# Natural Q by a transposing DMA: a two-block attention backward kernel on one core

## The chip, the core and the metric

The kernel runs on one core of one Trainium2 chip. The metric is the device time of one execution in microseconds. The core has a matrix engine (TensorE, PE in the profile, its weight loads PEld), a vector engine (VectorE, DVE), an activation engine (ScalarE, ACT), a general engine (GpSimd, POOL) and a sync engine (SyncE, SP) that here does nothing but issue DMAs. Sixteen DMA engines move the data between HBM (the chip's main memory) and SBUF (the on-chip buffer, 128 partitions). Matmuls write to PSUM, a small accumulator memory of eight banks, and ScalarE or VectorE must copy ("evict") the result from there into SBUF. A matmul contracts over the partitions of its two operands, so an operand whose contracted dimension lies along the free axis must first be transposed. That can be done by TensorE, with a matmul against an identity matrix and an eviction, or by a DMA that transposes.

## The reference

Two independent attention blocks, A and B, of the same shape: 8 batches (B), 96 queries (Sq), model width 640 (D), 32 heads (H), 512 keys (Sk), head width 128 (Dh), all in bfloat16. The kernel computes the forward output and the gradients of all ten inputs.

```
def _A_ref(x, k_cache, v_cache, wq, wo):
    q = (x @ wq).reshape(B, Sq, H, Dh).transpose(0, 2, 1, 3)
    scores = jnp.einsum("bhqd,bhkd->bhqk", q, k_cache) * (Dh ** -0.5)
    p = softmax(scores, axis=-1)
    o = jnp.einsum("bhqk,bhkd->bhqd", p, v_cache)
    return o.transpose(0, 2, 1, 3).reshape(B, Sq, H * Dh) @ wo
...
_out, _vjp = jax.vjp(_f, A_x, A_k_cache, ..., B_wo)   # _f: both blocks, joined on the last axis
return (_out, *_vjp(grad_out))
```

## The kernel before

One program does block A and then block B. Within a block it runs over the 32 heads, and within a head over the 8 batches. A head and batch together are a chunk; there are 2 x 32 x 8 = 512 chunks, and 64 heads counted through both blocks (head 8 here is the ninth head of block A, head 32 the first of block B).

**Order of the work.** The order is written by hand, in ticks. Each head h starts at tick `tick0 + 8 h`, and chunk b of it at one tick later each. Small functions are added to an emitter with a tick and a slot in the tick (lines 505 to 543) and run in that order. The table OFF (line 45) tells at which tick after its start a chunk's steps come, and HK (line 46) at which tick a head's steps come. The tile framework then gives each engine its own fixed queue of instructions, with semaphore waits where data or a buffer is not ready. Each engine takes its queue strictly in order, the sync engine's DMAs too: a DMA that waits holds all that stand behind it.

**A chunk**, by ticks: load K and V, 128 KB each, by the sync queue (`c_ld`, L235; 11 K buffers, 8 V buffers); transpose both on TensorE and evict them together (`c_s1`, L249, L251, L253); scores S = Q K^T (`c_s2a`, L265), row maximum, exponential (L277) and normalisation into P (L287, L296, GpSimd); transpose P, output O^T (`c_s45`, L312, L321); dV from P and natural dO (`c_s4`, L338), evicted by ScalarE into one of six dV_sb tiles (L340) and stored by the sync queue (L341); dP and the row sums, dS (`c_s6`, L360 to L364); dK from dS and natural Q (`c_s7`, L404), evicted (L406) and stored by the sync queue (L407); transpose dS, dQ^T (`c_s78`, L378, L387).

"Natural" means with the queries on the partitions. dK contracts over the queries, so it needs natural Q, while the scores need Q^T.

**A head** adds: the loads of its slice of wq and of wo, the latter transposed by a DMA (`pA`, L179, L181); Q^T and dO^T for all eight batches, two halves of 384 columns each (`pC`, L215, ticks -3 to 0); natural dO at ticks 1 and 2 and natural Q at ticks 3 and 4, by four TensorE transposes into a PSUM bank and one VectorE eviction for each half (`pD`, L231, L232, L170 in `evac`); a transposing DMA for wq^T (`pW`, L195); and, some ten ticks after the head began, two transposing DMAs of O^T and dQ^T (`qA`, L416, targets Onat and dQnat) followed by the weight gradients dwo (`qB`, L430) and dwq (`qD`, L450). All the transposing DMAs, all loads of K and V and all stores of dK and dV stand in the sync queue: 36 issues for a head. The wq loads and the weight gradients' stores go by GpSimd's queue.

**A group** is eight heads. When its last head is through, wo for the group is loaded (`gW`, L462, 1280 KB) and the output projections of the forward output and of dx run over 26 ticks (`gU`, L481), spread between the chunks of the next group's first heads. So of each eight heads some three or four carry projection matmuls, and the others ("plain heads") do not; the first group of all carries none. A group's results are summed in SBUF, and the last group of a block writes them out through four `ob` tiles (L491 to L493).

Of the kernel before, what the change touches and what calls it, by code (L numbers as in the profile page):

```python
# [11 lines left out]
BF16 = mybir.dt.bfloat16  # L12
# [28 lines left out]
SL_HEAD = 90  # L41
# [1 line left out]
SL_SETUP = 96  # L43

OFF = dict(ld=0, s1=2, s2=3, s3=3, s4=4, s5=5, s6=6, s7=7, s8=8)
HK = dict(pA=-6, pB=-4, pW=4, pC0=[-3, -2], pC1=[-1, 0], pD1=[1, 2], pD0=[3, 4], qA0=13, qA1=16, qB=[17, 18], qD=[(19, 0, 2), (20, 2, 4), (21, 4, 5)])
EV = dict(pB0="act", pB1="dve", pC00="act", pC01="act", pC10="act", pC11="dve", pD0="dve", pD1="dve", qA0="dve", qA1="dve", qB0="act", qB1="act", gU="act")
PRIO_OFF = 2000
GSPREAD = 26
# [3 lines left out]
def build_block(tc, em, tick0, blk, x, kc, vc, wq, wo, g_all, out_all, dx, dk, dv, dwq, dwo, ident, ones, pools, HG=8, first=True, groups=None):  # L53
    nc = tc.nc
    B, Sq, D = x.shape
    _, H, Sk, Dh = kc.shape
    assert Dh == 128 and Sk % 128 == 0 and D % 128 == 0
    T = B * Sq
# [3 lines left out]
    KC = Sk // 128  # L62
# [22 lines left out]
    const, ps, kvp, wk, hd, hst, grp = (pools[k] for k in ("const", "ps", "kvp", "wk", "hd", "hst", "grp"))  # L85

    def bank(shape, dt, name):
        return ps.tile(shape, dt, name=name, tag="bank")
# [3 lines left out]
    HS = pools["HS"]  # L92
# [72 lines left out]
    def evac(eng, dst, src, sc=None):  # L165
        if eng == "act":
            nc.scalar.activation(dst, src, ACT.Identity, scale=(1.0 if sc is None else sc))
        else:
            if sc is None:
                nc.vector.tensor_copy(dst, src)  # L170
            else:
                nc.vector.tensor_scalar(dst, src, float(sc), None, op0=ALU.mult)
# [12 lines left out]
    def pB(h):  # L185
        def f():
            st = HS[(blk, h)]
            st["QT_h"] = hd.tile([128, T], BF16, name="QT_h")
            st["dOT_h"] = hd.tile([128, T], BF16, name="dOT_h")
        return f  # L190

    def pW(h):
        def f():
            wqT_h = hst.tile([128, 1, D], BF16, name="wqT_h")
            tc.keep_in_program_order(nc.sync.dma_start_transpose(wqT_h[:], wq[:, h * 128:(h + 1) * 128]))  # L195
            HS[(blk, h)]["wqT_h"] = wqT_h[:, 0]
        return f

    def pC(h, which, si):
        def f():  # L200
            st = HS[(blk, h)]
            (t0, w) = tsplits[si]
            if which == 0:
                dst = st["QT_h"]
                lhs = lambda c: st["wq_h"][:, c, :]
                rhsT = S["xT"]
                sc = scale
            else:
                dst = st["dOT_h"]
                lhs = lambda c: st["woT_h"][:, c, :]  # L210
                rhsT = S["gT"]
                sc = None
            q_ps = bank([128, w], F32, "q_ps")
            for c in range(DC):
                nc.tensor.matmul(q_ps[:], lhs(c), rhsT[:, c, t0:t0 + w], start=(c == 0), stop=(c == DC - 1))  # L215
            evac(EV["pC%d%d" % (which, si)], dst[:, t0:t0 + w], q_ps[:], sc)
        return f

    def pD(h, which, half):
        def f():  # L220
            st = HS[(blk, h)]
            src = st["QT_h"] if which == 0 else st["dOT_h"]
            name = "Qnat_h" if which == 0 else "dOnat_h"
            if half == 0:
                st[name] = hd.tile([Sq, B * 128], BF16, name=name)
            b0 = half * HB
            nb = B - b0 if half else HB
            n_ps = bank([Sq, 8 * 128], BF16, "n_ps")
            for i in range(nb):
                b = b0 + i  # L230
                nc.tensor.transpose(n_ps[:, i * 128:(i + 1) * 128], src[:, b * Sq:(b + 1) * Sq], ident[:])  # L231
            evac(EV["pD%d" % which], st[name][:, b0 * 128:(b0 + nb) * 128], n_ps[:, 0:nb * 128])  # L232
        return f

    def c_ld(h, b):  # L235
# [22 lines left out]
    def c_s2a(h, b):  # L258
        def f():
            with tc.high_priority(PRIO_OFF):  # L260
                st = CS[(blk, h, b)]
                hs = HS[(blk, h)]
                tok = slice(b * Sq, (b + 1) * Sq)
                S_ps = bank([Sq, Sk], F32, "S_ps")
                nc.tensor.matmul(S_ps[:], hs["QT_h"][:, tok], st["KT"], start=True, stop=True)  # L265
                negm = wk.tile([Sq, 1], F32, name="negm", bufs=3)
                nc.vector.tensor_reduce(negm[:], S_ps[:], axis=AX.X, op=ALU.max, negate=True)  # L267
                st["S_ps"], st["negm"] = S_ps, negm
        return f
# [61 lines left out]
    def c_s4(h, b):  # L331
        def f():
            st = CS[(blk, h, b)]
            hs = HS[(blk, h)]
            P_sb = st["P_sb"]
            dV_ps = bank([128, KC * 128], F32, "dV_ps")
            for c in range(KC):
                nc.tensor.matmul(dV_ps[:, c * 128:(c + 1) * 128], P_sb[:, c * 128:(c + 1) * 128], hs["dOnat_h"][:, b * 128:(b + 1) * 128], start=True, stop=True)  # L338
            dV_sb = wk.tile([128, KC * 128], BF16, name="dV_sb", bufs=6)
            nc.scalar.activation(dV_sb[:], dV_ps[:], ACT.Identity, scale=1.0)  # L340
            nc.sync.dma_start(dv[b, h].rearrange("(p c) d -> p (c d)", c=KC), dV_sb[:])  # L341
        return f
# [54 lines left out]
    def c_s7(h, b):  # L397
        def f():
            st = CS[(blk, h, b)]
            hs = HS[(blk, h)]  # L400
            dS_sb = st["dS_sb"]
            dK_ps = bank([128, KC * 128], F32, "dK_ps")
            for c in range(KC):
                nc.tensor.matmul(dK_ps[:, c * 128:(c + 1) * 128], dS_sb[:, c * 128:(c + 1) * 128], hs["Qnat_h"][:, b * 128:(b + 1) * 128], start=True, stop=True)  # L404
            dK_sb = wk.tile([128, KC * 128], BF16, name="dK_sb", bufs=6)
            nc.scalar.activation(dK_sb[:], dK_ps[:], ACT.Identity, scale=1.0)  # L406
            nc.sync.dma_start(dk[b, h].rearrange("(p c) d -> p (c d)", c=KC), dK_sb[:])  # L407
        return f
# [62 lines left out]
    def gU(g, which, t, gi):  # L471
        def f():
            acc = S.get("out_acc" if which == 0 else "dx_acc")
            dst_flat = out_flat if which == 0 else dx_flat
            (c0, w) = gsplits[gi]
            o_ps = bank([128, w], F32, "o_ps")
            for hh in range(groups[g]):
                h = GH0[g] + hh
                src = HS[(blk, h)]["OT_h"] if which == 0 else HS[(blk, h)]["dQT_h"]
                rhs = G[g]["wo_r"][:, hh, c0:c0 + w] if which == 0 else HS[(blk, h)]["wqT_h"][:, c0:c0 + w]  # L480
                nc.tensor.matmul(o_ps[:], src[:, t * 128:(t + 1) * 128], rhs, start=(hh == 0), stop=(hh == groups[g] - 1))  # L481
            if NG == 1:
                ob = wk.tile([128, w], BF16, name="ob", bufs=4)
                evac(EV["gU"], ob[:], o_ps[:])
                nc.gpsimd.dma_start(dst_flat[t * 128:(t + 1) * 128, c0:c0 + w], ob[:])
            elif g == 0:
                evac(EV["gU"], acc[:, t, c0:c0 + w], o_ps[:])
            elif g < NG - 1:
                nc.vector.tensor_tensor(acc[:, t, c0:c0 + w], o_ps[:], acc[:, t, c0:c0 + w], op=ALU.add)
            else:  # L490
                ob = wk.tile([128, w], BF16, name="ob", bufs=4)  # L491
                nc.vector.tensor_tensor(ob[:], o_ps[:], acc[:, t, c0:c0 + w], op=ALU.add)
                (nc.gpsimd if first else nc.sync).dma_start(dst_flat[t * 128:(t + 1) * 128, c0:c0 + w], ob[:])  # L493
        return f
# [4 lines left out]
    for g in range(NG):  # L499
        h0 = GH0[g]  # L500
        for hh in range(groups[g]):
            h = h0 + hh
            c0t = tick0 + h * B
            em.add(c0t + HK["pA"], SL_LOAD, pA(h))
            em.add(c0t + HK["pB"], SL_HEAD, pB(h))
            em.add(c0t + HK["pW"], SL_HEAD, pW(h))
            for si in range(NTS):
                em.add(c0t + HK["pC0"][min(si, len(HK["pC0"]) - 1)], SL_HEAD, pC(h, 0, si))
                em.add(c0t + HK["pC1"][min(si, len(HK["pC1"]) - 1)], SL_HEAD, pC(h, 1, si))
            for half in range(2):  # L510
                em.add(c0t + HK["pD1"][half], SL_HEAD, pD(h, 1, half))
                em.add(c0t + HK["pD0"][half], SL_HEAD, pD(h, 0, half))
            for b in range(B):
                ct = c0t + b
                em.add(ct + OFF["ld"], SLOTS["LOAD"], c_ld(h, b))
# [143 lines left out]
```

## Time and profile before

| | before |
|---|---|
| device time, median of 3 runs | 1777.6 us (1771.38 to 1781.83) |
| profiled execution | 1778.72 us |
| its span, first to last instruction | 1776.9 us |
| mean granted TensorE clock | 0.995 of full |
| DMA | 370.73 MB, mean 209 GB/s, 508657 packets, of which 230000 under 512 B |
| Onat and dQnat transposes, issue to landing, median | 3.8 us (64 of each) |
| TensorE transposes of Q (L231, from QT_h) | 512, mean record 219 to 223 ns |
| evictions of natural Q (L170) | 128, mean 410 ns |

The profile is of one execution. Engines' busy times are unions of their instructions' records. A TensorE record covers the pipeline from the first operand to the last result, so records overlap, and what a matmul takes of the engine is the distance from its start to the next one's. The page counts no busy time for issuing DMAs; that is seen in the sync queue's own timeline, where the duration of an entry is the time the queue needs to hand over one DMA. "DMA share" is the mean share of time in which the 16 DMA engines have packets in flight; it can pass 1 where packets overlap. The chain of waits follows back what released the last instruction, and the clock column tells which share of TensorE's full clock was granted.

### The profile page before, as it was taken

The numbers are of one execution on the slowest core, as the hardware profiler recorded it, in microseconds if no ns is written. First come the engines' busy times: TensorE is split into PE (matmuls) and PEld (weight loads), VectorE is DVE, ScalarE is ACT, GpSimd is POOL, SyncE is SP. The second block draws the span as 40 slices with busy tenths as digits, with TensorE's granted clock in tenths as the row PEclk, the third lists the DMA queues.
The fourth block names the chain that finished last, engine by engine and source line by source line (L and its number), as shares of the span: only waits on it lengthen the run. The fifth ranks groups of instructions, "written<-read, shape, count | busy, mean of one in ns | idle before, by whom it ended". The sixth has DMA issues, their size and how long they took to land.

```text
span 1776.9 us, 65815 instructions
## 1 busy us (share of the span) xinstructions
PE 1752.8 (99%) x24538; PEld 1476.6 (83%) x24538; DVE 1449.4 (82%) x3106; ACT 1470.3 (83%) x4081; POOL 717.1 (40%) x1260
## 2 busy tenths in 40 slices
PE   8999899999999999999899999999999999999998
PEld 6888788888888888888788888888888888888886
DVE  7888766888878887788687888668987788878894
ACT  5999788899778987798777999789987799877992
POOL 2444433444334443345344444334443344433441
PEclk9999999999999999999899999999999999999999
DMA  8889975899858896689997799678896788867874
GB/s 212 220 221 221 240 191 167 206 217 237 210 168 214 217 245 186 178 209 223 236 254 188 211 222 248 186 178 208 221 245 183 182 219 225 238 179 174 222 215 128
DMA packets 508657, 370.73 MB, mean 209 GB/s; under 512 B 230000, under 2 KB 497136, under 8 KB 508336
## 3 DMA queue, kind: packets, MB, share of 16 engines
q1 hardware_dynamic: 493072, 319.82, 70.5%
q0 software_dynamic: 15264, 46.71, 8.8%
q8 instruction: 192, 3.15, 0.8%
q14 instruction: 129, 1.06, 0.2%
HBM read 160.10 MB, written 159.12 MB: 180 GB/s over the span
## 4 chain that ended last, share of the span: by engine, by line
PE 97%; DMA 2%; DVE 1%; issue 0%; ACT 0%; POOL 0%; SPq 0%; ACTq 0%; DVEq 0%; POOLq 0%
PE q_ps L215 12%; PE o_ps L481 12%; PE dK_ps L404 6%; PE dV_ps L338 6%; PE kvT_ps L249 6%; PE kvT_ps L251 6%; PE dP_ps L360 6%; PE S_ps L265 6%; PE dwq_ps L450 6%; PE dwo_ps L430 6%; PE dq_dst_ps L387 5%; PE optp_ps L321 5%; PE optp_ps L312 5%; PE dq_dst_ps L378 5%; PE n_ps L231 4%; DMA xT<-in_B_x_dram 1%
## 5 line engine op out<-in xcount | busy, mean ns | idle before, releaser
L296 POOL TENSOR_SCALAR P_sb<-E_sb,rinv 96x512 bf16<-96x512 bf16 x512 | 352.3, 688 | 680.6 <-DVE rinv L287 674.7
L277 ACT ACTIVATE E_sb<-S_ps,negm 96x512 bf16<-96x512 f32 x512 | 348.7, 681 | 152.1 <-DVE negm L267 151.4
L364 DVE SCALAR_TENSOR_TENSOR dS_sb<-dP_ps,dl_ps,P_sb 96x512 bf16<-96x512 f32 x512 | 384.7, 751 | 106.6 <-PE dl_ps L362 97.6
L267 DVE TENSOR_REDUCE negm<-S_ps 96x1 f32<-96x512 f32 x512 | 348.2, 680 | 56.7 <-PE S_ps L265 55.1
L253 DVE COPY KVT<-kvT_ps 128x1024 bf16<-128x1024 bf16 x512 | 348.5, 681 | 18.5 <-PE kvT_ps L251 6.3
L406 ACT ACTIVATE dK_sb<-dK_ps 128x512 bf16<-128x512 f32 x512 | 302.9, 592 | 51.9 <-PE dK_ps L404 48.5
L340 ACT ACTIVATE dV_sb<-dV_ps 128x512 bf16<-128x512 f32 x512 | 315.6, 616 | 0.0
L327 ACT ACTIVATE PT_sb<-optp_ps 128x384 bf16<-128x384 bf16 x512 | 254.3, 497 | 0.0
L350 POOL TENSOR_TENSOR prod<-OT_h,dOT_h 128x96 bf16<-128x96 bf16 x512 | 186.8, 365 | 106.4 <-ACT OT_h L324 87.4
L249 PE MATMUL kvT_ps<-ident,K_sb 128*128 128x128 bf16 x2048 | 198.4, 219 | 0.0
L251 PE MATMUL kvT_ps<-ident,V_sb 128*128 128x128 bf16 x2048 | 198.4, 219 | 0.0
L404 PE MATMUL dK_ps<-Qnat_h,dS_sb 96*128 96x128 bf16 x2048 | 198.4, 219 | 0.0
L338 PE MATMUL dV_ps<-dOnat_h,P_sb 96*128 96x128 bf16 x2048 | 198.1, 219 | 0.0
L265 PE MATMUL S_ps<-KVT,QT_h 128*96 128x512 bf16 x512 | 194.3, 380 | 1.2 <-DVE KVT L253 1.2
L360 PE MATMUL dP_ps<-KVT,dOT_h 128*96 128x512 bf16 x512 | 195.5, 382 | 0.0
L249 PEld LDWEIGHTS <-K_sb 128*128 128x128 bf16 x2048 | 152.1, 98 | 37.2 <-issue 2.0
L389 DVE COPY dST_sb<-dq_dst_ps 128x384 bf16<-128x384 bf16 x512 | 178.9, 349 | 2.1 <-PE dq_dst_ps L387 1.6
L321 PE MATMUL optp_ps<-ident,P_sb 96*128 96x96 bf16 x2048 | 171.9, 205 | 2.4 <-POOL P_sb L296 2.3
L387 PE MATMUL dq_dst_ps<-ident,dS_sb 96*128 96x96 bf16 x2048 | 172.5, 206 | 0.8 <-DVE dS_sb L364 0.4
L312 PE MATMUL optp_ps<-PT_sb,V_sb 128*128 128x96 bf16 x2048 | 172.5, 206 | 0.0
L378 PE MATMUL dq_dst_ps<-dST_sb,K_sb 128*128 128x96 bf16 x2048 | 171.1, 206 | 0.0
L450 PE MATMUL dwq_ps<-dQnat,x_nat 128*128 128x128 bf16 x1920 | 160.3, 220 | 5.0 <-DMA dQnat<-dQT_h 5.0
(71 smaller groups left out, 3560.3 us busy)
## 6 DMA issues: line engine op xcount, KB each, us to landing
out_dram<-dV_sb SPq DMA_DIRECT2D x512, 128.0 KB, 2.6
out_dram<-dK_sb SPq DMA_DIRECT2D x512, 128.0 KB, 2.6
K_sb<-in_A_k_cache_dram SPq DMA_DIRECT2D x256, 128.0 KB, 2.8
V_sb<-in_A_v_cache_dram SPq DMA_DIRECT2D x256, 128.0 KB, 2.7
K_sb<-in_B_k_cache_dram SPq DMA_DIRECT2D x256, 128.0 KB, 2.6
V_sb<-in_B_v_cache_dram SPq DMA_DIRECT2D x256, 128.0 KB, 2.6
out_dram<-dwo_sb POOLq DMA_DIRECT2D x64, 160.0 KB, 3.0
out_dram<-dwq_sb POOLq DMA_DIRECT2D x64, 160.0 KB, 3.2
```

The source lines that it names most:

```text
L249: nc.tensor.transpose(kvT_ps[:, c * 128:(c + 1) * 128], st["K_sb"][:, c, :], ident[:])
L251: nc.tensor.transpose(kvT_ps[:, Sk + c * 128:Sk + (c + 1) * 128], st["V_sb"][:, c, :], ident[:])
L253: nc.vector.tensor_copy(KVT[:], kvT_ps[:])
L267: nc.vector.tensor_reduce(negm[:], S_ps[:], axis=AX.X, op=ALU.max, negate=True)
L277: nc.scalar.activation(E_sb[:], st["S_ps"][:], ACT.Exp, bias=st["negm"][:], scale=1.0, accum_out=rowsum[:])
L296: nc.gpsimd.tensor_scalar(P_sb[:], st["E_sb"][:], st["rinv"][:], 0.0, op0=ALU.mult, op1=ALU.add)
L338: nc.tensor.matmul(dV_ps[:, c * 128:(c + 1) * 128], P_sb[:, c * 128:(c + 1) * 128], hs["dOnat_h"][:, b * 128:(b + 1) * 128], start=True, s ...
L340: nc.scalar.activation(dV_sb[:], dV_ps[:], ACT.Identity, scale=1.0)
L360: nc.tensor.matmul(dP_ps[:], hs["dOT_h"][:, tok], st["VT"], start=True, stop=True)
L364: nc.vector.scalar_tensor_tensor(dS_sb[:], dP_ps[:], dl_ps[:, 0:1], st["P_sb"][:], op0=ALU.subtract, op1=ALU.mult)
L404: nc.tensor.matmul(dK_ps[:, c * 128:(c + 1) * 128], dS_sb[:, c * 128:(c + 1) * 128], hs["Qnat_h"][:, b * 128:(b + 1) * 128], start=True, s ...
L406: nc.scalar.activation(dK_sb[:], dK_ps[:], ACT.Identity, scale=1.0)
```

## The change

Natural Q is no longer made by TensorE and VectorE. Q^T is stored in 128-column slots, one for each batch, of which the first 96 columns hold the queries and the other 32 are set to zero by GpSimd when the tile is taken (tick -4). The evictions of Q^T write into the slots, and the score matmul reads the first 96 columns of a slot. One tick before the head's first chunk, a single DMA on the sync queue transposes all 1024 columns, and natural Q arrives as eight slots of 128 partitions, of which the dK matmul reads the first 96. Natural dO is made as before. Two buffer counts go down: dV tiles from six to five, output tiles from four to three.

```
-HK = dict(..., pD1=[1, 2], pD0=[3, 4], qA0=13, ...)
+HK = dict(..., pD1=[1, 2], pN=-1, qA0=13, ...)
...
     def pB(h):
-            st["QT_h"] = hd.tile([128, T], BF16, name="QT_h")
+            st["QT_h"] = hd.tile([128, B, 128], BF16, name="QT_h")
+            nc.gpsimd.memset(st["QT_h"][:, :, Sq:128], 0.0)
             st["dOT_h"] = hd.tile([128, T], BF16, name="dOT_h")
...
     def pC(h, which, si):
+            b0 = t0 // Sq
             if which == 0:
-                dst = st["QT_h"]
+                dst = st["QT_h"][:, b0:b0 + w // Sq, 0:Sq]
...
-                dst = st["dOT_h"]
+                dst = st["dOT_h"][:, t0:t0 + w].rearrange("p (b q) -> p b q", q=Sq)
...
-            evac(EV["pC%d%d" % (which, si)], dst[:, t0:t0 + w], q_ps[:], sc)
+            evac(EV["pC%d%d" % (which, si)], dst, q_ps[:].rearrange("p (b q) -> p b q", q=Sq), sc)
...
-    def pD(h, which, half):
+    def pD(h, half):
...
-                nc.tensor.transpose(n_ps[:, i * 128:(i + 1) * 128], src[:, b * Sq:(b + 1) * Sq], ident[:])
-            evac(EV["pD%d" % which], st[name][:, b0 * 128:(b0 + nb) * 128], n_ps[:, 0:nb * 128])
+                nc.tensor.transpose(n_ps[:, i * 128:(i + 1) * 128], st["dOT_h"][:, b * Sq:(b + 1) * Sq], ident[:])
+            evac("dve", st["dOnat_h"][:, b0 * 128:(b0 + nb) * 128], n_ps[:, 0:nb * 128])
...
+    def pN(h):
+        def f():
+            st = HS[(blk, h)]
+            st["Qnat_h"] = hd.tile([128, B, 128], BF16, name="Qnat_h")
+            tc.keep_in_program_order(nc.sync.dma_start_transpose(st["Qnat_h"][:], st["QT_h"][:].rearrange("p b q -> p (b q)")))
+        return f
...
-                nc.tensor.matmul(S_ps[:], hs["QT_h"][:, tok], st["KT"], start=True, stop=True)
+                nc.tensor.matmul(S_ps[:], hs["QT_h"][:, b, 0:Sq], st["KT"], start=True, stop=True)
...
-            dV_sb = wk.tile([128, KC * 128], BF16, name="dV_sb", bufs=6)
+            dV_sb = wk.tile([128, KC * 128], BF16, name="dV_sb", bufs=5)
...
-                nc.tensor.matmul(dK_ps[...], dS_sb[...], hs["Qnat_h"][:, b * 128:(b + 1) * 128], start=True, stop=True)
+                nc.tensor.matmul(dK_ps[...], dS_sb[...], hs["Qnat_h"][0:Sq, b, :], start=True, stop=True)
...
-                ob = wk.tile([128, w], BF16, name="ob", bufs=4)
+                ob = wk.tile([128, w], BF16, name="ob", bufs=3)
...
             for half in range(2):
-                em.add(c0t + HK["pD1"][half], SL_HEAD, pD(h, 1, half))
-                em.add(c0t + HK["pD0"][half], SL_HEAD, pD(h, 0, half))
+                em.add(c0t + HK["pD1"][half], SL_HEAD, pD(h, half))
+            em.add(c0t + HK["pN"], SL_HEAD, pN(h))
```

More of the change, by code (lines that the diff above doesn't have):

```diff
@@ L45 @@
 OFF = dict(ld=0, s1=2, s2=3, s3=3, s4=4, s5=5, s6=6, s7=7, s8=8)
-HK = dict(pA=-6, pB=-4, pW=4, pC0=[-3, -2], pC1=[-1, 0], pD1=[1, 2], pD0=[3, 4], qA0=13, qA1=16, qB=[17, 18], qD=[(19, 0, 2), (20, 2, 4), (21, 4, 5)])
+HK = dict(pA=-6, pB=-4, pW=4, pC0=[-3, -2], pC1=[-1, 0], pD1=[1, 2], pN=-1, qA0=13, qA1=16, qB=[17, 18], qD=[(19, 0, 2), (20, 2, 4), (21, 4, 5)])
 EV = dict(pB0="act", pB1="dve", pC00="act", pC01="act", pC10="act", pC11="dve", pD0="dve", pD1="dve", qA0="dve", qA1="dve", qB0="act", qB1="act", gU="act")
@@ L215, in f @@
                 nc.tensor.matmul(q_ps[:], lhs(c), rhsT[:, c, t0:t0 + w], start=(c == 0), stop=(c == DC - 1))
-            evac(EV["pC%d%d" % (which, si)], dst[:, t0:t0 + w], q_ps[:], sc)
+            evac(EV["pC%d%d" % (which, si)], dst, q_ps[:].rearrange("p (b q) -> p b q", q=Sq), sc)
         return f
-    def pD(h, which, half):
+    def pD(h, half):
         def f():
             st = HS[(blk, h)]
-            src = st["QT_h"] if which == 0 else st["dOT_h"]
-            name = "Qnat_h" if which == 0 else "dOnat_h"
             if half == 0:
-                st[name] = hd.tile([Sq, B * 128], BF16, name=name)
+                st["dOnat_h"] = hd.tile([Sq, B * 128], BF16, name="dOnat_h")
             b0 = half * HB
@@ L403, in f @@
             for c in range(KC):
-                nc.tensor.matmul(dK_ps[:, c * 128:(c + 1) * 128], dS_sb[:, c * 128:(c + 1) * 128], hs["Qnat_h"][:, b * 128:(b + 1) * 128], start=True, stop=True)
+                nc.tensor.matmul(dK_ps[:, c * 128:(c + 1) * 128], dS_sb[:, c * 128:(c + 1) * 128], hs["Qnat_h"][0:Sq, b, :], start=True, stop=True)
             dK_sb = wk.tile([128, KC * 128], BF16, name="dK_sb", bufs=6)
@@ L490, in f @@
             else:
-                ob = wk.tile([128, w], BF16, name="ob", bufs=4)
+                ob = wk.tile([128, w], BF16, name="ob", bufs=3)
                 nc.vector.tensor_tensor(ob[:], o_ps[:], acc[:, t, c0:c0 + w], op=ALU.add)
```

## The prediction

> **What bounds the kernel now.** I read the page's engine shares and chain first, then a table of windows (one window per head, cut where a head's first K transpose starts), then the timelines of TensorE and of the sync queue (SP).
>
> ```profile
> PE 1752.8 (99%) x24538; PEld 1476.6 (83%) x24538; DVE 1449.4 (82%) x3106; ACT 1470.3 (83%) x4081; POOL 717.1 (40%) x1260
> PE 97%; DMA 2%; DVE 1%; issue 0%; ACT 0%; POOL 0%; SPq 0%; ACTq 0%; DVEq 0%; POOLq 0%
> ```
>
> TensorE is busy 99% and is 97% of the chain. Alone, that says: each matmul removed shortens the kernel. The windows (us, then busy us and count of PE, PEld, DVE, ACT, POOL, then clock, DMA share, GB/s) say where this may stop. Two are of heads without output projections, then one of the head in which wo_r is loaded, one with projections:
>
> ```profile
> 1254.40:1278.20 23.80, 23.80 (x360) 20.49 (x358) 21.29 (x47) 22.36 (x63) 10.78 (x19) 1.00 0.89 215
> 1278.20:1302.10 23.90, 23.90 (x361) 20.52 (x360) 21.39 (x47) 22.37 (x63) 11.10 (x20) 1.00 0.92 226
> 1302.10:1329.20 27.10, 27.10 (x385) 22.85 (x383) 23.12 (x50) 23.09 (x64) 11.39 (x20) 1.00 0.96 258
> 1361.70:1393.20 31.50, 31.50 (x417) 26.06 (x415) 24.87 (x53) 23.20 (x63) 10.82 (x19) 1.00 0.72 177
> ```
>
> A plain head takes 23.8 us with the DMA engines 0.9 busy; a head with projections 30 to 32.5 us at about 0.7. In a plain head the sync queue, which no line of the page counts as an engine, looks like this (start, duration):
>
> ```profile
> 1289.50 0.38 SPq L407 DMA_DIRECT2D out_dram<-dK_sb  x1
> 1289.97 1.22 SPq L416 DMA_TRANSPOSE Onat<-OT_h  x1
> 1291.28 1.55 SPq L341 DMA_DIRECT2D out_dram<-dV_sb  x1
> 1292.89 1.19 SPq L195 DMA_TRANSPOSE wqT_h<-in_B_wq_dram  x1
> 1294.17 0.53 SPq L239 DMA_DIRECT2D K_sb<-in_B_k_cache_dram  x1
> 1294.79 0.38 SPq L240 DMA_DIRECT2D V_sb<-in_B_v_cache_dram  x1
> ```
>
> Each issue starts about 0.09 us after the one before it ended: the queue waits for nothing, it is behind. A head needs 36 issues (32 loads and stores, 4 transposes); the plain heads from 327 to 1720 us hold some 34 to 36 each. Pairing the n-th K load with TensorE's last dQ matmul of chunk n-11 (which frees its buffer; 11 buffers) gives the queue's lateness: at the first chunk of heads 44 to 49 it is 1.8, 3.2, 3.7, 5.2, 6.1, 8.6 us, and 1.5 in head 50, after two heads with projections. The other groups of eight heads do the same. So TensorE is fed from a lead that plain heads eat up. Once, in head 8, it ran out. The queue's and TensorE's timelines there:
>
> ```profile
> 198.78 2.06 SPq L416 DMA_TRANSPOSE dQnat<-dQT_h  x1
> ```
>
> ```profile
> 203.78 0.40 PE L231 MATMUL n_ps<-ident,QT_h 128*96 128x128 bf16 x4
> 209.22 0.29 PE L450 MATMUL dwq_ps<-dQnat,x_nat 128*128 128x128 bf16 x1 [5.04 <-DMA dQnat<-dQT_h]
> ```
>
> and the window behind it:
>
> ```profile
> 209.30:213.30 4.00, 4.00 (x39) 3.72 (x40) 2.03 (x5) 1.28 (x4) 0.44 (x1) 0.50 1.12 352
> ```
>
> TensorE stood 5.04 us for a late transposing DMA, and then ran 4 us at a granted clock of 0.50.
>
> **Part by part.** *Removed from TensorE:* 512 transposes of Q (L231). The row's mean of 219 ns is latency; the price is start to start:
>
> ```profile
> 573.05 0.40 PE L231 MATMUL n_ps<-ident,QT_h 128*96 128x128 bf16 x4
> 573.29 0.22 PE L450 MATMUL dwq_ps<-dQnat,x_nat 128*128 128x128 bf16 x1
> ```
>
> Four take 0.24 us, two such fours a head, 0.48 us. The first step of a four is 72 ns against 56 because the short dl matmul stands before it; the next matmul inherits that 16 ns, so 0.45 us a head, 64 x 0.45 = **-29 us** (bounds -29 and -31), if nothing else holds TensorE.
>
> *Removed from VectorE:* 128 evictions of 410 ns, 0.82 us a head. VectorE is busy 21.3 of 23.8, off the chain: 0.
>
> *Added on GpSimd:* 64 memsets of 128x256. Nearest rows: 205 ns for 128x128, 688 ns for its 96x512 operation; about 0.3 us. It waits for the S matmuls and the Q transpose of two heads before, both long done. P_sb and prod queue behind it; GpSimd is busy 10.8 of 23.8, which covers it: 0 (uncovered 64 x 0.3 = 19).
>
> *Q written in 128-column slots:* same 128x384 eviction (514 ns) with gaps in its target; I take the same. ACT has 1.4 us idle in a plain head for two of them, if they get dearer.
>
> *Added on the sync queue:* 64 transposing DMAs of 128x1024. In the changed program's queue order each stands behind a head's dQnat transpose and one dV store, ahead of a K load, a dK store, a V load, a dV store and woT's transpose. Its own wait (Q's evictions a tick earlier, the memset) is met when the queue is behind. Its data are due at the head's first dK, seven ticks later, so it is never late itself. What it costs is the queue's time. Nearest row, the SBUF to SBUF transposes of 128x768 (Onat, dQnat): lowest 1.22; in the plain heads from 1230.6 to 1302.1 the medians are 1.96 and 1.36, the longest 2.8. I take 1.66, for these are the heads that count, plus the gap of 0.09 and 0.15 for the next issue (0.53 instead of 0.38 after a transpose): 1.9 us (bounds 1.46 and 3.05). In heads with projections the queue has time and it costs nothing.
>
> On the DMA engines: the packet records hold 184,704 packets of 256 bytes, the 261 transposes, of 31 ns each; 1024 more a head are 1024 x 31 / 16 = 2.0 us. A plain head at 0.90 of 23.8 uses 21.4, then 23.4, which is all of a 23.35 us head. The Trainium skill ("Advanced Engine Details and Errata", X-Bar Transpose) says that trn2's transposing DMAs are as fast as regular ones; at the 52 ns of this trace's 1024-byte packets that would be 256 x 52 / 16 = 0.83 us. The rows show 2.4 times that, and the rows decide. The skill's "DMA: Bandwidth & Descriptors" (Issuing engines are not separate DMA queues) calls the issue time usually small against the transfer. By that rule the sum would end at -29; here the issues alone fill the plain heads.
>
> *Where the stall goes.* In a plain head the queue falls behind by 1.9 more, and TensorE asks 0.45 sooner: 2.35 us a head (bounds 1.9 and 3.5). Before, the least time by which a load or transpose landed ahead of its use was, group by group: 0 in head 8 (the stall above), then 0.9, 2.5, 4.4, 1.2, 1.5, 3.8 in heads 16, 24, 32, 40, 48, 56, and 6.7 in head 63. Before head 8 seven plain heads run; before the others the four plain heads and half the next, less about 0.8 in which the queue still waits: 3.7 heads (3.2 at the end). Stalls: 7 x 2.35 = 16.5, then 3.7 x 2.35 = 8.7 less each lead: 7.8, 6.2, 4.3, 7.5, 7.2, 4.9, and 0.8. Sum **+55** (at 1.9: +41; at 3.5: +93). What is late next: dQnat's product and the K transposes; all of TensorE's order waits behind them. Then the heads with projections catch up (32 us against about 27 of queue), so each group pays anew.
>
> *dV tiles five:* pairing each dV eviction with the landing of the store five before leaves 1.6 us in the group of head 8, 2.5 or more elsewhere. It binds at about the same lateness as the loads, so it adds nothing of its own (bound: 1 us a group, 7). *Output tiles three:* pairing at the end leaves 0.1 us instead of 1.2; 0 (bound 1).
>
> Sum against the profiled execution (span 1776.9, 1778.7 with what lies around it): 1778.7 - 29 + 55 = 1804.7. The median shown is 1.1 lower: **1804 us**.
>
> **Rivals.** (1) *TensorE stays the only bound:* the queue's long issues (1.55 for a store that else takes 0.38) are slack that the new DMA merely fills. For it: the page's chain has 2% DMA. Against it: lateness grows in every plain head although only 1 in 12 plain issues is long. 1777.6 - 29 = 1749. (2) *The stalls only give the gain back:* the transpose costs its lowest (e 1.9), and half the lateness is made up within plain heads because stalled stretches leave the DMA engines free: about 41 x 0.6 = 25, so 1774. (3) *The DMA engines become the bound:* at 23.4 of 23.35 us the issues lengthen as in the longest rows, 3.5 us a head: 1777.6 - 29 + 93 = 1841. It decides once issues over 1 us pass one in five. (4) *The memset holds GpSimd:* P_sb late, 64 x 0.3 = 19 uncovered, 1767; the idle of 13 us a head speaks against it.
>
> **How the numbers follow.** Forecast (queue late, 1789 to 1841 by its bounds, 1804) 0.58; rival 1 0.18; rival 2 0.14; rival 3 0.07; rival 4 0.03. A measurement here tells about 0.5% from no change (9 us: 1768.7 to 1786.5). Faster: rivals 1 and 4 and a bit of 2, 0.22. Same: most of rival 2 and the forecast's low edge, 0.16. Slower: 0.62. The range 1752 to 1838 leaves out about half of rival 1 and of rival 3; the likeliest case alone has 1789 to 1841.
>
> **What would show it.** Right: TensorE's idle before kvT (K_sb, V_sb) and dwq (dQnat) grows from 5 us to some 50, in head 8 and at each later group's first head, with the granted clock near 0.5 after the long ones; plain heads early in a group at 23.35 us; Qnat's issues near 1.7 us with no gap around them; heads with projections 0.45 us shorter. Wrong: plain heads of 23.35 us throughout a group and no DMA wait (rival 1); or issues that are back to back yet short, with lateness growing less than 2 us a head.

## The result, and the profile after

The changed kernel takes 1824.9 us (median of 4 runs, 1822.5 to 1826.0), the kernel before 1778.8 us in the same series: a ratio of 1.026, 95% interval 1.023 to 1.030. Ratios compare fast executions alone; medians take in the few that came out over 1.5% above the fastest of their kernel. The execution profiled has a span of 1822.2 us, 45.3 more than before. These lines of its page answer to those shown of before: engines, chain of waits, and the three groups in which TensorE stands (busy us, mean ns | idle before, releaser).

```profile
PE 1743.2 (96%) x24026; PEld 1459.0 (80%) x24026; DVE 1410.6 (77%) x2978; ACT 1457.4 (80%) x4081; POOL 735.0 (40%) x1324
PE 90%; DMA 8%; ACT 1%; DVE 1%; issue 0%; SPq 0%; POOL 0%; ACTq 0%; DVEq 0%; POOLq 0%
...
L256 PE MATMUL kvT_ps<-ident,K_sb 128*128 128x128 bf16 x2048 | 200.1, 221 | 10.9 <-DMA K_sb<-in_A_k_cache_dram 7.7
L258 PE MATMUL kvT_ps<-ident,V_sb 128*128 128x128 bf16 x2048 | 200.4, 221 | 8.2 <-DMA V_sb<-in_A_v_cache_dram 5.9
L457 PE MATMUL dwq_ps<-dQnat,x_nat 128*128 128x128 bf16 x1920 | 165.0, 224 | 39.8 <-DMA dQnat<-dQT_h 39.5
```

TensorE has 512 instructions less and is busy 9.6 us less, yet DMA is now 8% of the chain instead of 2%. The wait for dQnat alone is 39.5 us; before, it was 5.0, once. The new transpose itself, Qnat, is in none of these lines: nothing waits for its data.

Windows of the changed kernel (us, busy us and count of PE, PEld, DVE, ACT, POOL, then clock, DMA share, GB/s): two plain heads, the stretch of the longest stall, the 4 us after it.

```profile
1256.70:1280.00 23.30, 23.30 (x352) 20.00 (x350) 20.68 (x45) 21.97 (x63) 10.97 (x20) 1.00 0.77 217
1280.00:1303.40 23.40, 23.40 (x352) 20.02 (x351) 20.79 (x45) 21.97 (x63) 11.01 (x20) 1.00 0.99 210
652.60:664.00 11.40, 5.05 (x81) 4.37 (x78) 5.28 (x12) 5.73 (x16) 3.56 (x7) 0.84 1.02 232
664.10:668.10 4.00, 3.97 (x46) 3.70 (x47) 1.71 (x4) 1.51 (x4) 0.07 (x1) 0.62 1.11 254
```

Plain heads that don't stall take 23.35 us, 0.49 less than before: TensorE gives the time back as forecast. In the stretch of the stall it is busy 5 of 11.4 us, and in the 4 us afterwards it gets 0.62 of its clock.

The timelines around that stall, first the sync queue (start, duration), then TensorE (what ended the wait in brackets):

```profile
654.36 2.43 SPq L423 DMA_TRANSPOSE dQnat<-dQT_h  x1
656.88 1.68 SPq L348 DMA_DIRECT2D out_dram<-dV_sb  x1
658.66 3.98 SPq L239 DMA_TRANSPOSE Qnat_h<-QT_h  x1
662.73 0.53 SPq L246 DMA_DIRECT2D K_sb<-in_A_k_cache_dram  x1
```

```profile
657.48 0.16 PE L369 MATMUL dl_ps<-ones,prod 128*96 128x1 bf16 x1
664.13 0.29 PE L457 MATMUL dwq_ps<-dQnat,x_nat 128*128 128x128 bf16 x1 [6.48 <-DMA dQnat<-dQT_h]
```

TensorE wanted dQnat at 657.65 us, 3.3 us after its issue began. Before, the same head's transpose (issued at 636.0, wanted at 644.8) had 8.8 us. And it landed later: in the DMA view of this stretch after 9.7 us, of the same stretch before after 4.0. Both views, after and then before (KB, us from issue to landing):

```profile
wo_r<-in_A_wo_dram POOLq DMA_DIRECT2D x1, 1280.0 KB, 9.6
...
dQnat<-dQT_h SPq DMA_TRANSPOSE x1, 9.7
```

```profile
wo_r<-in_A_wo_dram POOLq DMA_DIRECT2D x1, 1280.0 KB, 8.5
...
dQnat<-dQT_h SPq DMA_TRANSPOSE x1, 4.0
```

The stretch holds the group's 1280 KB load of wo_r, from GpSimd's queue. Before, dQnat's transpose was issued at 636.0, ahead of that load (639.3); after, at 654.4, behind it (652.2). The same holds group by group. Before, only the transpose of the one stall, in head 8, stood behind the load and landed in 10.4 us; the seven others stood ahead of it and landed in 2.5 to 4.8. After, six stand 2.1 to 5.3 us behind it and land in 6.2 to 9.7, the last stands 0.4 us ahead of it and lands in 10.6, and one, 5.8 us ahead, in 3.9.

Added up over the whole trace, TensorE's waits of over 0.15 us are 71.2 us (before 16.3; the one ahead of its first matmul is left out in both), so **+55**. The steps from one matmul's start to the next, where they are far longer than their kind's median, hold 32 us beyond the median and the waits (before 10.8), **+21**. Of these, 24 us (before 5.5) lie where the granted clock is 0.50, so some 18 of the 21 are half clock; the rest is mostly what a step with a wait takes beyond the wait itself. (The clock's record begins 12 us into the run; in it the clock is at 0.50 for 71.7 us, before for 19.3.) With 64 heads of 0.49 us less, -31 + 55 + 21 = +45, the 45.3 by which the spans differ.

### The profile page after: what moved, and what is told of

It reads as the page before. It is cut to its first block, busy times and chain, and to the rows that moved or that the text cites. A ratio compares the mean times of both kernels' runs of the same rounds, so it can differ in the third digit from the quotient of the medians.

```text
span 1822.2 us, 64863 instructions
## 1 busy us (share of the span) xinstructions
PE 1743.2 (96%) x24026; PEld 1459.0 (80%) x24026; DVE 1410.6 (77%) x2978; ACT 1457.4 (80%) x4081; POOL 735.0 (40%) x1324
## 4 chain that ended last, share of the span: by engine, by line
PE 90%; DMA 8%; ACT 1%; DVE 1%; issue 0%; SPq 0%; POOL 0%; ACTq 0%; DVEq 0%; POOLq 0%
PE q_ps L217 12%; PE o_ps L488 11%; PE dwq_ps L457 6%; PE kvT_ps L258 6%; PE dK_ps L411 6%; PE kvT_ps L256 6%; PE S_ps L272 6%; PE dV_ps L345 6%; PE dP_ps L367 6%; PE dwo_ps L437 5%; DMA dQnat<-dQT_h 5%; PE dq_dst_ps L394 5%; PE dq_dst_ps L385 5%; PE optp_ps L319 5%; PE optp_ps L328 5%; PE n_ps L231 2%
## 5 line engine op out<-in xcount | busy, mean ns | idle before, releaser
L256 PE MATMUL kvT_ps<-ident,K_sb 128*128 128x128 bf16 x2048 | 200.1, 221 | 10.9 <-DMA K_sb<-in_A_k_cache_dram 7.7
L457 PE MATMUL dwq_ps<-dQnat,x_nat 128*128 128x128 bf16 x1920 | 165.0, 224 | 39.8 <-DMA dQnat<-dQT_h 39.5
L457 PEld LDWEIGHTS <-x_nat 128*128 128x128 bf16 x1920 | 129.2, 100 | 80.1 <-DMA dQnat<-dQT_h 38.3
L256 PEld LDWEIGHTS <-K_sb 128*128 128x128 bf16 x2048 | 152.9, 99 | 50.0 <-DMA K_sb<-in_A_k_cache_dram 10.6
```

The lines of the kernel that those rows point to most:

```text
L256: nc.tensor.transpose(kvT_ps[:, c * 128:(c + 1) * 128], st["K_sb"][:, c, :], ident[:])
L457: nc.tensor.matmul(w_ps[:, ci * 128:(ci + 1) * 128], S["x_nat"][:, t, c * 128:(c + 1) * 128], dQnat[:, t, :], start=(t == 0), stop=(t == T ...
```

## The experiments

Three theories are told apart: the sync queue's issue time is the price (the issue theory, **Q** below), the DMA engines' packets are (**D**), or the buffer counts are (**B**). Later a fourth came, **W**: the load of wo_r takes part in it. Where "before" stands beside a result, it ran on the same chip.

**1. The buffer counts alone** (kernel before).

```
-dV_sb = wk.tile(..., bufs=6)     -ob = wk.tile(..., bufs=4)
+dV_sb = wk.tile(..., bufs=5)     +ob = wk.tile(..., bufs=3)
```

> The kernel before, with dV tiles five and output tiles three and nothing else of the change. Late queue theory: both counts bind only when the sync queue is later than it is in the kernel before, so 1777 to 1783 us. Rival, the buffers are the cause: ScalarE's dV evictions wait for their stores and a large part of the 46 us appears, 1795 us or more.

1780.4 us, before 1777.7: ratio 1.002 (0.999 to 1.005). B falls.

**2. The change without its transposing DMA.**

```
-st["Qnat_h"] = hd.tile(...); nc.sync.dma_start_transpose(st["Qnat_h"][:], ...)
+st["Qnat_h"] = one tile of zeros, made once, for all heads
```

> The changed kernel without the 64 transposing DMAs: natural Q is one tile of zeros for all heads (dK then comes out zero); slots, memsets, buffer counts and the removed TensorE transposes stay. Late queue theory: the whole gain of the removed transposes appears, 29 us, and the sync queue is as late as before plus 0.45 us a plain head; with one stall in head 8 of 5 to 9 us that is 1746 to 1755 us. Rival, the memset, the slots or the buffers cost the time: 1790 us or more.

1764.8 us, ratio 0.993 (0.989 to 0.996): 60 us below the changed kernel, so the DMA is the cost. But it is 10 us above the expectation: only 13 of the 29 us come out. In its profile TensorE waits 13.9 us for dQnat:

```profile
PE dwq_ps L459 <- DMA dQnat<-dQT_h: 13.9, 4, 6.2
```

(Total us, times, longest; before it was 5.0, once. The runs spread from 1754.9 to 1776.8 us, and the one profiled took 1757.4.) A faster TensorE alone already asks sooner than the queue can serve.

**3 and 4. An extra transposing DMA in the kernel before**, of 768 and of 128 columns, into a tile that nothing reads, at the place where the change has its own, with the buffer counts of the change. TensorE's work is that of before.

```
+xt = hd.tile([128, XB, 128], BF16, name="xdst", bufs=1)      # XB = 6, then 1
+nc.sync.dma_start_transpose(xt[:], HS[(blk, h)]["QT_h"][:, 0:XB * 128])
```

> The kernel before with the buffer counts of the change and, in the place in the sync queue where the change puts it, one more transposing DMA a head, 128x768, whose result nobody reads; TensorE keeps its transposes of Q. Late queue theory: 1.9 us more of queue a plain head; stalls of some 41 us and some 15 us of TensorE at half clock behind them, 1815 to 1845 us, with dwq's waits for dQnat in the first plain group and at the first heads of later groups. Rival, the cost lies in the matmul side (slots, padded operands, the order of TensorE): about 1778 us.

> As the run with the extra 128x768 transposing DMA, but only 128 columns, so a sixth of the packets (0.25 us instead of 1.5 us of the 16 DMA engines a head). If the queue's issue time is what counts (1.2 us and the gaps, the same for 640 and 768 columns): 1.45 us a plain head, stalls of some 28 us and 10 us at half clock, 1800 to 1825 us. If the DMA engines' time is what counts: 1778 to 1787 us.

768 columns: 1821.7 us, ratio 1.027 (1.022 to 1.031). 128 columns: 1821.1 us, ratio 1.025 (1.019 to 1.031). A sixth of the packets, the same loss. The tile view of the second (ns, lowest, median, highest; then us to landing) shows what did not shrink:

```profile
L239 SPq DMA_TRANSPOSE xdst<-QT_h x64: 1100/1120/2759, 15.7 to 1765.7; - x64
...
DMA to landing us min/median/max: 2.2/2.5/7.6
```

The 768-column one issues in 1.21 us, the 128-column one in 1.12. D falls: packets went down by six and nothing came back. Q stands: the loss goes with the issue time.

**5 to 7. The issues taken off the sync queue elsewhere**: dK's stores by GpSimd's queue, of every second chunk (5) or of all (6), in the changed kernel; and all in the kernel before (7). The bytes are the same.

```
-nc.sync.dma_start(dk[b, h]..., dK_sb[:])
+(nc.gpsimd if b % 2 else nc.sync).dma_start(dk[b, h]..., dK_sb[:])   # 5
+nc.gpsimd.dma_start(dk[b, h]..., dK_sb[:])                           # 6, 7
```

> The changed kernel with the dK stores of odd batches issued by GpSimd instead of the sync queue: four issues a head less on that queue (4 x 0.47 = 1.9 us), the same bytes on the DMA engines. Issue theory (the run with 128 columns cost as much as the one with 768): the queue is then as late as without the transposing DMA, so 1752 to 1772 us, as in the run without it (1764.8). Rival, the DMA engines' load is what makes the queue late: 1810 to 1828 us.

> The changed kernel with all dK stores issued by GpSimd: eight issues a head less on the sync queue (3.8 us), the same bytes. Issue theory: the queue needs less than a plain head's 23.35 us, lateness does not build up, TensorE's waits for dQnat, K and V vanish, in the first group too: 1738 to 1756 us, below both kernels. It would be spoilt if GpSimd, which takes some 0.6 to 0.9 us for an issue and waits for each dK eviction in its own queue, delivers P_sb and prod late: then waits of TensorE on P_sb, 1760 to 1790 us. Rival, the DMA engines' load: 1800 us or more.

> The kernel before with all dK stores issued by GpSimd. Issue theory: only the stall of head 8 and its half clock go (7 us), and some at the block boundary: 1765 to 1773 us. The difference to the changed kernel with the same stores is then the gain of the removed transposes, 25 to 31 us. Rival: 1778 us and no difference between the two.

Half the stores: 1765.8 us, ratio 0.991 (0.988 to 0.994). All: **1741.4 us**, ratio 0.979 (0.977 to 0.981), the fastest kernel of the study, ahead of both. The kernel before with all stores moved: 1768.5, ratio 0.993 (0.991 to 0.995). All three times fall as Q expected. The page of the sixth, and TensorE's longest waits in it:

```profile
PE 1719.1 (99%) x24026; PEld 1442.2 (83%) x24026; DVE 1410.4 (81%) x2978; ACT 1453.3 (84%) x4081; POOL 1022.6 (59%) x1836
```

```profile
PE q_ps L217 <- DMA xT<-in_B_x_dram: 5.9, 3, 2.6
PE tp_ps L129 <- DMA x_nat<-in_A_x_dram: 4.1, 1, 4.1
PE optp_ps L328 <- POOL P_sb L303: 2.4, 5, 1.1
```

No dQnat, K_sb or V_sb is left among the waits, with the transposing DMA and all its packets in place. The queue's lateness no longer builds up: at the first chunks of heads 44 to 48 it is 1.4, 3.1, 2.7, 4.0 and 2.8 us, where the changed kernel goes from 0.9 to 10.9. GpSimd pays 0.59 us for each of 512 stores and has the room: 59% busy. The difference between the sixth and the seventh, 27 us, is what the removed TensorE transposes are worth when the queue is not in the way.

**8. The dwq products two ticks later** (changed kernel): is dQnat's place the fault, or only where the lateness shows?

```
-qD=[(19, 0, 2), (20, 2, 4), (21, 4, 5)]
+qD=[(21, 0, 2), (22, 2, 4), (23, 4, 5)]
```

> The changed kernel with the dwq products two ticks (6 us) later, so that dQnat is due later; nothing else moved. Late queue theory: dQnat's waits (39.5 us of the profile) mostly go, but the queue is as late as before, so that K and V loads land too late instead: 1805 to 1826 us. Rival, the due time of dQnat is the trouble and the queue's lateness harmless: 1770 us or less.

1840.9 us, ratio 1.034 (1.032 to 1.037), slower than the changed kernel and 15 us above the expectation. TensorE's longest waits:

```profile
PE kvT_ps L256 <- DMA K_sb<-in_A_k_cache_dram: 19.1, 7, 6.8
PE kvT_ps L256 <- DMA K_sb<-in_B_k_cache_dram: 13.9, 4, 5.0
PE optp_ps L328 <- POOL P_sb L303: 13.0, 33, 1.3
PE kvT_ps L258 <- DMA V_sb<-in_A_v_cache_dram: 6.3, 8, 3.8
```

The waits for dQnat are gone and those for K took their place: dQnat was the first to show the lateness. Two costs had not been foreseen: P_sb's 13 us (2.3 in the changed kernel), and steps beyond their median of 48 us (32). Those are not half clock: only 22 us of them (24 in the changed kernel) lie at a granted clock of 0.50, and 14 of the others are 79 steps at full clock in which the transpose of dS starts right after dS_sb is done: waits for VectorE that the overlap of the records hides.

**9. Qnat's transpose four ticks later** (`pN=3` for `pN=-1`, changed kernel).

> The changed kernel with the transposing DMA of Q issued at tick 3 of the head instead of one tick ahead of it: still four ticks before the first dK needs it, but no longer right behind dQnat's transpose and ahead of woT's. Issue theory: a late queue is as late wherever in a head the 1.9 us stand, 1805 to 1835 us. Rival, three transposing DMAs close together are the trouble: 1795 us or less.

1832.2 us, ratio 1.031 (1.027 to 1.035). The rival falls: in the other place the loss is there too, 7 us larger, but its waits are others. Now Qnat's own data come late:

```profile
PE dK_ps L411 <- DMA Qnat_h<-QT_h: 30.1, 15, 4.1
PE dwq_ps L457 <- DMA dQnat<-dQT_h: 27.9, 6, 9.7
```

**10. Four small plain copies in place of the transpose** (kernel before, with the buffer counts of the change): 128x128 each, SBUF to SBUF, unread. Is it transposing as such?

```
+for j in range(4):
+    nc.sync.dma_start(xt[:, j, :], HS[(blk, h)]["QT_h"][:, j * 128:(j + 1) * 128])
```

> The kernel before with the buffer counts of the change and, a tick ahead of each head, four plain copies of 128x128 from SBUF to SBUF on the sync queue, whose result nobody reads (4 x 0.47 = 1.9 us of issue, about 0.25 us each of the DMA engines by the packets of 256 bytes, no transposing). Issue theory: as late as with the extra transposing DMA, 1808 to 1835 us. Rival, it is the transposing that costs (the transposes hold each other or the queue up): 1776 to 1792 us.

1878.3 us, ratio 1.057 (1.052 to 1.062), 43 us above the top of what was expected. The four took 2.4 us together (by the median), not four times 0.38:

```profile
L240 SPq DMA_DIRECT2D xdst<-QT_h x256: 465/599/2336, 14.9 to 1828.2; - x128
```

The edit also changed the queue's order: V loads came to stand behind a store and woT's transpose, and TensorE waited 44.1 us for V. So a loss as large comes without any more transposing, which speaks against transposing as such; but how much of it is issue time and how much the new order this run cannot tell.

**11 and 12. The load of wo_r moved** (W). In the changed kernel five ticks earlier; in the kernel before two ticks earlier, so that it stands ahead of dQnat's transpose as it does after the change. Neither touches the sync queue's or TensorE's order.

```
-em.add(cLg + OFF["s5"] - 2, SL_LOAD, gW(g))
+em.add(cLg - 2, SL_LOAD, gW(g))       # 11, changed kernel
+em.add(cLg + 1, SL_LOAD, gW(g))       # 12, kernel before
```

> The changed kernel, with wo_r's load of 1280 KB (GpSimd's queue) emitted five ticks earlier, between two dQnat transposes; the orders of the sync queue and of TensorE stay as they are. In the changed kernel's trace the dQnat transpose that TensorE waits for is issued 2 to 5 us behind that load and lands 6.2 to 10.6 us after its issue; in the kernel before it is issued 1.4 to 5.9 us ahead of it (but for head 8) and lands in 2.5 to 4.8. Theory L (the sync queue's lateness alone makes the stalls): moving the load changes nothing of it, 1815 to 1830 us, dQnat waits of 35 to 40 us. Theory W (the lateness puts the transpose behind the load, and half of each stall is its slower landing): dQnat lands in 3 to 5 us in the groups' first heads, its waits there shrink by some 5 us in six groups, to about 10 us in all, the K and V waits of about 19 us stay, and with less half clock the time is 1780 to 1805.

> The kernel before, with wo_r's load emitted two ticks (some 6 us) earlier, so that it is issued ahead of the dQnat transpose of each group, as it is in the changed kernel; the sync queue has not one instruction more. Theory L: as before, 1772 to 1784 us, one dQnat wait of 5 us in head 8. Theory W: dQnat lands in 6 to 10 us in the groups' first heads instead of 2.5 to 4.8; the leads that were 2.1, 4.8, 3.2 and 2.9 us in the groups of heads 16, 24, 40 and 48 turn into waits of 1 to 3 us each, and with the half clock after them the time is 1780 to 1792.

The eleventh: 1812.5 us, ratio 1.018 (1.012 to 1.023), between the two forecasts and 12 us under the changed kernel. The dQnat transposes that stood behind the load now land in 2.8 to 5.3 us, and no wait for them is left. But TensorE still waits 28.1 us for dQnat (39.5 in the changed kernel), for the load met the late transpose of the head before: that one lands in 7.1 to 10.8 us in six groups. The DMA view around 617 to 635 us, where TensorE stood 3.96 us for it:

```profile
wo_r<-in_A_wo_dram POOLq DMA_DIRECT2D x1, 1280.0 KB, 11.8
...
dQnat<-dQT_h SPq DMA_TRANSPOSE x1, 9.2
```

The twelfth: 1782.2 us, ratio 1.0025 (1.0002 to 1.0048); the time fits both theories, the trace does not. The DMA view of 634 to 650 us, and TensorE's waits:

```profile
dQnat<-dQT_h SPq DMA_TRANSPOSE x1, 9.6
```

```profile
PE dwq_ps L450 <- DMA dQnat<-dQT_h: 5.6, 4, 2.1
```

With the load beside or ahead of it the transpose lands in 7.2 to 10.9 us in six groups, though the queue has not one issue more. In head 8 the load now stands far ahead: the transpose lands in 3.2 us and its stall of 5.04 is gone, but TensorE waits 3.5 us for K there instead. So the time nearly stays, while new waits of 1.3 to 2.1 us came in the groups of heads 16, 24 and 40, three of the four that W named.

W holds in part: the slow landing goes wherever the load goes. Run 5 says the same without moving the load: its three dQnat transposes that are issued behind it, by 0.7 to 1.4 us, land in 9.4 to 11.7 us and make all of the 19.3 us that TensorE waits for dQnat there; the five ahead of it land in 2.8 to 5.7, and nothing waits for them. In run 6 all eight stand 5.9 to 8.3 us ahead of the load. W is not the whole: in the twelfth it costs a few us, for in the kernel before the queue leaves 5.4 to 11.3 us between such a transpose's issue and its use. It takes a late queue to make it dear.

## Why the prediction came out as it did

The forecast case came true: slower, by stalls of a late sync queue. The time lies 21 us above the 1804 predicted and inside the range.

- **TensorE's gain, -29 us: right.** Plain heads take 23.35 us, 0.49 less (31 us in 64 heads); the medians of runs 6 and 7 differ by 27 us.
- **The sum of the stalls, +55: right in size; its working only in part.** By group the forecast was 16.5, 7.8, 6.2, 4.3, 7.5, 7.2, 4.9 and 0.8 us; the longer waits for dQnat, K and V (over 0.5 us, and 0.23 in the second group) came to 14.4 (5.0 of it there before), 4.2, 6.5, 5.3, 6.5, 6.8, 6.6 and 5.4. But the lateness grew less than the 2.35 us a plain head that was put in: at the first chunks of heads 44 to 48 it is 0.9, 3.1, 6.4, 9.4, 10.9 us, 2.5 a head against 1.1 before, so 1.4 more. (In head 47 TensorE itself already stood, which gives the queue time; up to there it is 2.8 against 1.1, so 1.7 more.) What filled the gap, as far as the traces show, is W, which the prediction missed: it took each lead with its landing time of before, while a later transpose falls behind wo_r's load and lands some 5 us later. In head 24, 5.5 us of lead went to the later issue (8.8 to 3.3) and 5.7 to the slower landing (4.0 to 9.7). That the two errors met at +55 is partly luck.
- **Half clock after the stalls: the mis-sized term, priced at nothing, some 18 us of the +21.** The prediction showed a window at 0.50 behind a stall of 5 us and left it out of the sum. The Trainium skill ("TensorE: Matmul & The Clock Gate", the table of clock states) gives half clock after an idle window of about 3.4 us; the 0.62 behind the 6.48 us stall agrees in kind. Shorter waits did it here as well: behind the one of 2.81 us in head 4 the granted clock is 0.50 from 110.7 to 114.1 us.
- **The queue's price, 1.9 us a head (1.66 for the issue): too high where it counts.** The forecast's sign, Qnat's issues near 1.7 us, did not come. The source view of the changed kernel has a median of 1.23 (lowest, median, highest in ns):

```profile
L239 SPq DMA_TRANSPOSE Qnat_h<-QT_h x64: 1231/1234/4967, 17.2 to 1753.6; - x64
```

  The mean of the 64 is 1.57 us, but the longest, 3.4 to 5.0, are those of heads 8, 24, 40 and 56, right behind the late dQnat transpose and beside wo_r's load. The 19 issued in plain heads from head 12 on have a mean of 1.38, which with the same 0.09 and 0.15 makes 1.6 a head, not 1.9. Of the queue's issues 90.5% follow within 0.15 us, before 83.5%: part of the price went into gaps that were there.
- **Never late itself: right.** Qnat lands at least 3.9 us ahead of the first dK; four ticks later it would not (run 9).
- **Buffers 0, memset 0: right for the buffers** (run 1; ScalarE waits 2.6 us in all for dV tiles). The memset was not run alone; POOL is 40% busy after as before and no wait names it.
- **Rival 1** (slack hides the issue) **and rival 2** (the stalls only give the gain back) fell by the time; run 2 shows why the first could not be: the gain itself empties the lead.
- **Rival 3** (the DMA engines) fell though its time, 1841, was not far. Its condition, more than one issue in five over 1 us, was not met: over 1 us are 18.6% of all issues (before 15.8%), and most of these are the transposing ones, which always are; of the plain ones it is 5.9% (5.2%). Run 4 has the loss without the packets, run 6 the packets without the loss. (The forecast's 2.4 times is packets of 256 bytes against packets of 1024. The plain 256-byte packets of run 10 take 18 ns on average where no transpose is in flight, the transposing ones 30: at the same size it is 1.7 times.) Where the DMA engines' load may count is the stretch of wo_r's load (W); that their packets are the reason for the slow landing there is not shown.
- The Trainium skill ("DMA: Bandwidth & Descriptors", Issuing engines are not separate DMA queues) calls the issue time that a second queue saves usually small against the DMA. A store's issue is, 0.38 us against 2.9 from issue to landing (medians, changed kernel); but a head of the changed kernel needs 37 of them on one queue. Here moving 512 issues to a second queue was worth 83 us (1824.9 to 1741.4).

Not tried: splitting wo_r's load into parts, and the wo_r shift together with the moved stores. How the +76 us of stalls and half clock divide between lateness and W is known only from the 12 us of run 11, which put the load onto another late transpose, so W's full share stays open.

## What to carry to other kernels

Treat the queue that issues the DMAs as an engine: here 0.47 us for a plain issue and its gap, 1.2 and more for a transposing one of 128 columns, 1.3 of 1024; where the issues of a stage fill it, any DMA added or any engine made faster turns into waits. Before trading engine work for a DMA, move plain stores to the queue of an engine that has room, and look which large load a delayed transfer will then fall behind. Price a stall at more than its length: here 55 us of new waits brought some 18 us of half clock.

## What the runs showed of the hardware

- A transposing DMA's issue time hardly depends on its size: 1.12 us for 128 columns, 1.21 for 768, 1.23 for 1024 (medians).
- A plain SBUF to SBUF copy of 128x128 issues in 0.60 us (median), longer than a 128 KB load or store at 0.38 to 0.41 (kernel before).
- Issued up to 5.3 us behind a 1280 KB load of another queue, a transposing DMA of 128x768 lands in 6.2 to 10.4 us (dQnat, both kernels); the median of all is 3.8.
- The granted clock fell to 0.50 for 3.4 us behind a wait of TensorE of 2.81 us.
- GpSimd's queue takes 0.59 us for a 128 KB store, at any point of the run (0.54 to 0.62), while the sync queue's stores of the same size stretch from 0.33 to 2.5 us in the changed kernel, and its longest issue (Qnat's) to 5.0.
